# Decoding float64 weights in an attention and feed-forward kernel: magnitudes made in the final weight tile, low words converted on GpSimd

## The chip, the cores and the metric

The kernel runs on one core of a Trainium2 chip. The metric is the device time of one execution in microseconds; the time before is the median of three runs. A core has five engines that work in parallel, each through its own queue in order: TensorE (PE, with its weight loads PEld), VectorE (DVE), ScalarE (ACT), GpSimd (POOL) and SyncE (SP), which here starts the DMA transfers. They wait for each other on semaphores.

## What is computed

Attention over 8 batches of 8 heads, 576 positions, head dimension 64, that keeps for each query the 32 largest scores; then, on the 4608 rows that it gives, a feed-forward layer with an ELU.

```python
scores = scale * np.matmul(q, k.transpose(0, 1, 3, 2))
kth = np.partition(scores, -top_k, axis=-1)[..., -top_k:-top_k + 1]
mask = scores >= kth
...
attn = np.exp(scores)
attn = attn / (np.sum(attn, axis=-1, keepdims=True) + 1e-09)
...
h = x @ w_in
g = np.where(h > 0.0, h, alpha * (np.exp(np.minimum(h, 0.0)) - 1.0))
return (g @ w_out).astype(np.float32)
```

q, k and v are float32. The weights w_in (512 x 2048) and w_out (2048 x 512) come as float64, which the engines do not compute in: the kernel reads each weight as two 32-bit words and makes a float32 of them.

## The kernel before

*Attention.* The work is cut into steps; a step is one tile of 128 queries and one pair of heads. For each, PE makes the scores (L299), ACT copies them to a tile `sc` (L307), and DVE finds the 32 largest by four MAX8 and three MATCH_REPLACE8 per head (L318 to L328, in later steps L341 to L353). POOL makes two small numbers from the result, the neg and gap pair (L366, L368), ACT masks with them (Prelu, L369) and takes the exponential with its sum (L370). POOL normalises: five small instructions (L380 to L385), then two that scale the tile (L387). PE turns the normalised tile (L406), ACT copies the turned parts to `et` (L407), PE multiplies with v (L432), ACT copies the result to `xT` (L459).

*Feed-forward.* The rows are gathered in blocks of one to three tiles of 128 rows. A block has 16 hidden pieces (PE L504 with w_in; ACT L514, L517, L519; DVE L476 closes the ELU) and four projection pieces per tile (PE L529 with w_out). `feed` hands these pieces out among the attention steps by a plan of due times, and holds a piece back until as many weight pieces are decoded as it needs.

*Decoding.* The weights are cut into 32 pieces of 128 x 512, 16 of w_in, then 16 of w_out. A piece is loaded by SP into a `raw` tile of 1024 words (L153; seven buffers), low and high words in turn. Then, before the change:

- ACT L174 copies the low words to floats in place, times 2^-35 plus 2^17: the low word's top three bits become the last bits of the float.
- ACT L175 writes the sign of the value, as an 8-bit float, into the top byte of each low word.
- ACT L178 takes the absolute value of the high word, read as a float, times 2^-62, in place.
- POOL L179 clips that between two bounds, in place.
- DVE L186 shifts the high word left by three bits, in place.
- POOL L187 adds low and high words as integers into the final tile, `w_in` or `w_out`.

The first four are in `convert_first`, the last two in `convert_last`, called three pieces later. `decode_piece(i)` also issues the load of piece i + 3. The selection on DVE calls `hook` after MAX8s (L330, L354), four times per step, and each call runs one decode piece; so the 32 pieces and the three calls that empty the pipeline are spread over the first nine steps. A raw buffer is free for a new load once its piece's add is done, seven pieces earlier.

*Order.* In the first eight steps (`n < tight`) a scheduler orders the instructions of each engine; the start before them and everything after them keeps the order in which it is written. So the decoding lies in the part whose order the scheduler chooses, and a change to it can change the order of other work there too.

Of the kernel before, what the change touches and what calls it, by code (L numbers as in the profile page):

```python
# [8 lines left out]
AF = mybir.ActivationFunctionType  # L9
ALU = mybir.AluOpType  # L10
FP32 = mybir.dt.float32
U32 = mybir.dt.uint32
I32 = mybir.dt.int32
# [68 lines left out]
def kernel(  # L82
# [9 lines left out]
    nc = tc.nc  # L92
# [9 lines left out]
    NF = dff // P  # L102
# [3 lines left out]
    scale = 1.0 / float(D) ** 0.5  # L106
# [33 lines left out]
    raw = {}  # L140

    def weight(i):
        per = dff // WN
        if i < NC * per:
            f, c = divmod(i, NC)
            src = moe_w_in[c * P : (c + 1) * P, 2 * f * WN : 2 * (f + 1) * WN]
            return src, w_in[:, c, f * WN : (f + 1) * WN]
        f = i - NC * per
        return moe_w_out[f * P : (f + 1) * P, :], w_out[:, f, :]

    def load_weight(i):
        t = rawpool.tile([P, 2 * WN], U32, tag="raw", name="raw")
        nc.sync.dma_start(t[:], weight(i)[0])  # L153
        raw[i] = t

    def parts(t):
        words = t[:].rearrange("p (n w) -> p n w", w=2)
        signs = t[:].bitcast(FP8).rearrange("p (n w) -> p n w", w=8)
        return words[:, :, 0], words[:, :, 1], signs[:, :, 3]

    def convert_first(i):

        lo, hi, sign = parts(raw[i])
        ef, mf = hi.bitcast(FP32), lo.bitcast(FP32)
        nc.scalar.activation(mf, lo, AF.Copy, scale=2.0**-35, bias=2.0**17)  # L174
        nc.scalar.activation(  # L175
            sign, ef, AF.Sign, scale=2.0**64, bias=1.0, saturate=False
        )
        nc.scalar.activation(ef, ef, AF.Abs, scale=2.0**-62)  # L178
        nc.gpsimd.tensor_scalar(  # L179
            ef, ef, (2.0 - 2.0**-3 - 2.0**-23) * 2.0**-46, 2.0**-77, ALU.min, ALU.max  # L180
        )

    def convert_last(i):
        t, dst = raw.pop(i), weight(i)[1]
        lo, hi, sign = parts(t)
        nc.vector.tensor_single_scalar(hi, hi, 3, ALU.logical_shift_left)  # L186
        nc.gpsimd.tensor_tensor(  # L187
            dst.bitcast(I32), hi.bitcast(I32), lo.bitcast(I32), ALU.add
        )

    decode = []
    decoded = [0]
# [10 lines left out]
            late["x"] = ctx.enter_context(tc.tile_pool(name="xt", bufs=2))  # L203

    def decode_piece(i):
        if i < 2 * NF:
            if i + 3 < 2 * NF:
                load_weight(i + 3)
            convert_first(i)
        if i > 2:  # L210
            convert_last(i - 3)
            decoded[0] = i - 2

    loaded, kqT, vT = {}, {}, {}

# [342 lines left out]
    for b in range(B):  # L558
# [12 lines left out]
        for qt in range(J + 1):  # L571
# [8 lines left out]
            t = Tile(b, qt, rows, blk, slice(c0, c0 + n))  # L580
# [66 lines left out]
    for hp in range(1, NHP):  # L647
        load_v(0, hp)
    decode += [lambda i=i: decode_piece(i) for i in range(2 * NF + 3)]
    at(0, start_qk, 0, 2)  # L650
    at(1, start_qk, 0, 3)
# [93 lines left out]
```

## Time and profile before

| | us |
|---|---|
| median of three runs | 1667.17 (1666.97 to 1669.18) |
| the profiled execution | 1667.02 |
| its span, first to last instruction | 1665.2 |
| PE busy in the span | 1592.8 (96%) |
| DVE busy | 1495.8 (90%) |
| ACT busy | 1165.1 (70%) |
| POOL busy | 630.5 (38%) |
| mean granted TensorE clock | 0.977 of full speed |

A busy share is an average over stages with different limits. In the first 150 us weights are decoded, the granted TensorE clock lies between 0.5 and 1.0, and PE and DVE have gaps; in the 1400 us after that both are busy almost throughout; at the end PE works alone. Where a line of the trace gives a start and a length, both are in microseconds from the start of the span; `x2` is two instructions in a row, `[2.41 <-DVE m L328]` says that the engine sat idle for 2.41 us before it and that the DVE instruction of line 328 on tile `m` ended the wait. A line of a tile's instructions gives the shortest, median and longest duration in ns, then the first and last start. A line of stages gives the bounds of the stage, its length, the busy time of each engine with its number of instructions, the granted TensorE clock, the busy share of the DMA engines and what they moved in GB/s.

### The profile page before, as it was taken

The numbers are of one execution on the slowest core, as the hardware profiler recorded it, in microseconds if no ns is written. First come the engines' busy times: TensorE is split into PE (matmuls) and PEld (weight loads), VectorE is DVE, ScalarE is ACT, GpSimd is POOL, SyncE is SP. The second block draws the span as 40 slices with busy tenths as digits, with TensorE's granted clock in tenths as the row PEclk, the third lists the DMA queues.
The fourth block names the chain that finished last, engine by engine and source line by source line (L and its number), as shares of the span: only waits on it lengthen the run. The fifth ranks groups of instructions, "written<-read, shape, count | busy, mean of one in ns | idle before, by whom it ended". The sixth has DMA issues, their size and how long they took to land.

```text
span 1665.2 us, 25986 instructions
## 1 busy us (share of the span) xinstructions
PE 1592.8 (96%) x8528; PEld 1031.5 (62%) x8528; DVE 1495.8 (90%) x3044; ACT 1165.1 (70%) x2377; POOL 630.5 (38%) x1719
## 2 busy tenths in 40 slices
PE   5589999999999999999999999999999999999999
PEld 3366677657574767656566676755557575755565
DVE  5887999999999999999999999999999999998500
ACT  6998777668686777678667685868758585857521
POOL 3775444333334334333334333333333343332200
PEclk9578999999999999999999999999999999999999
DMA  7540120001100110001100111001200100000000
GB/s 211 171 144 7 23 50 29 7 15 44 48 1 8 43 42 22 1 28 37 42 14 1 50 29 35 1 14 43 50 13 1 28 15 29 7 7 7 7 13 13
DMA packets 101126, 56.21 MB, mean 34 GB/s; under 512 B 84096, under 2 KB 92288, under 8 KB 100992
## 3 DMA queue, kind: packets, MB, share of 16 engines
q1 hardware_dynamic: 99792, 54.26, 11.7%
q8 instruction: 68, 1.11, 0.3%
q14 instruction: 66, 0.54, 0.1%
q10 hardware_dynamic: 1200, 0.30, 0.1%
HBM read 45.09 MB, written 9.44 MB: 33 GB/s over the span
## 4 chain that ended last, share of the span: by engine, by line
PE 65%; DVE 21%; ACT 9%; POOL 3%; issue 2%; SPq 0%; DMA 0%; ACTq 0%; POOLq 0%; DVEq 0%
PE ops L529 24%; PE hps L504 20%; DVE wk L346 9%; DVE m L353 8%; PE avps L432 7%; PE scps L299 6%; PE eps L406 5%; DVE m L341 3%; ACT sc L370 2%; ACT sc L369 1%; DVE gT L476 1%; ACT raw L175 1%; PE qkps L269 1%; ACT et L407 1%; POOL w_in L187 1%
## 5 line engine op out<-in xcount | busy, mean ns | idle before, releaser
L353 DVE MAX8 m<-wk 128x8 f32<-128x576 f32 x816 | 577.0, 750 | 0.0
L504 PE MATMUL hps<-xT,w_in 128*128 128x256 f32 (+2 forms) x2432 | 548.1, 374 | 12.5 <-ACT xT L459 12.3
L529 PE MATMUL ops<-w_out,gT 128*128 128x512 f32 x1152 | 522.8, 598 | 0.0
L504 PEld LDWEIGHTS hps<-xT,w_in 128*128 128x128 f32 x2432 | 406.5, 193 | 109.2 <-issue 23.8
L346 DVE MATCH_REPLACE8 wk<-m,wk 128x576 f32<-128x576 f32 x544 | 400.8, 746 | 0.0
L529 PEld LDWEIGHTS ops<-w_out,gT 128*128 128x128 f32 x1152 | 208.7, 190 | 233.0 <-issue 219.5
L380 POOL TENSOR_SCALAR dene<-den 128x2 f32<-128x2 f32 x144 | 35.9, 249 | 771.2 <-ACT sc L370 770.6
L369 ACT ACTIVATE sc<-sc,neg 128x576 f32<-128x576 f32 x288 | 226.8, 788 | 89.2 <-POOL neg L366 89.0
L370 ACT ACTIVATE sc<-sc,gap 128x576 f32<-128x576 f32 x288 | 224.1, 778 | 25.7 <-ACT sc L369 0.7
L387 POOL TENSOR_SCALAR sc<-sc,rec 128x576 f32<-128x576 f32 x288 | 221.0, 778 | 14.9
L307 ACT ACTIVATE sc<-scps 128x576 f32<-128x576 f32 x288 | 174.0, 659 | 73.3 <-PE scps L299 73.3
L299 PE MATMUL scps<-kqT 64*128 64x288 f32 (+1 forms) x1280 | 201.8, 440 | 21.2 <-ACT kqT L275 7.9
L407 ACT COPY et<-eps 128x512 f32<-128x512 f32 x288 | 166.8, 579 | 55.2 <-PE eps L406 55.0
L346 DVE MATCH_REPLACE8 wk<-m,sc 128x576 f32<-128x576 f32 x272 | 200.4, 746 | 0.0
L432 PE MATMUL avps<-et,vT 128*64 128x256 f32 (+2 forms) x2080 | 193.3, 326 | 4.8 <-ACT et L407 4.6
L406 PEld LDWEIGHTS eps<-ident,sc 128*128 128x128 f32 x1152 | 143.6, 144 | 83.8 <-issue 46.2
L476 DVE SCALAR_TENSOR_TENSOR gT<-n,gT 128x512 f32<-128x512 f32 (+1 forms) x132 | 100.2, 759 | 102.0 <-ACT n L519 101.9
L341 DVE MAX8 m<-sc 128x8 f32<-128x576 f32 x272 | 191.8, 748 | 0.0
L406 PE MATMUL eps<-ident,sc 128*128 128x128 f32 x1152 | 175.7, 278 | 15.4 <-POOL sc L387 13.0
L432 PEld LDWEIGHTS avps<-et,vT 128*64 128x64 f32 x2080 | 122.6, 141 | 79.1 <-issue 22.8
L299 PEld LDWEIGHTS scps<-kqT 64*128 64x128 f32 (+1 forms) x1280 | 108.1, 181 | 91.9 <-issue 44.2
L514 ACT ACTIVATE n<-hps 128x512 f32<-128x512 f32 (+1 forms) x156 | 88.0, 564 | 71.4 <-PE hps L504 67.5
(47 smaller groups left out, 1170.2 us busy)
## 6 DMA issues: line engine op xcount, KB each, us to landing
kin<-in_k_dram SPq DMA_DIRECT2D x64, 128.0 KB, 2.8
raw<-in_moe_w_in_dram SPq DMA_DIRECT2D x16, 512.0 KB, 5.4
vT<-in_v_dram SPq DMA_DIRECT2D x64, 128.0 KB, 2.3
raw<-in_moe_w_out_dram SPq DMA_DIRECT2D x16, 512.0 KB, 3.9
out_dram<-osb SPq DMA_DIRECT2D x32, 256.0 KB, 2.3
qin<-in_q_dram SPq DMA_DIRECT2D x62, 128.0 KB, 2.8
kin<-in_k_dram SPq DMA_DIRECT2D x32, 32.0 KB, 2.4
vT<-in_v_dram SPq DMA_DIRECT2D x64, 16.0 KB, 2.2
```

Source lines behind the costliest of these rows:

```text
L299: nc.tensor.matmul(wide[i][rows, half, 0:HS], kq[part, q0 : q0 + u.t.ql], kq[part, k0 : k0 + HS], start=True, stop=True,)
L341: nc.vector.max(found[i], cur[i])
L346: nc.vector.match_replace(wk[i], found[i], cur[i], TAKEN)
L353: nc.vector.max(found[i], cur[i])
L369: nc.scalar.activation(sc, sc, AF.Prelu, bias=neg[:], alpha=STEEP)
L370: nc.scalar.activation(sc, sc, AF.Exp, bias=gap[:], accum_out=u.den[:, i : i + 1])
L387: nc.gpsimd.tensor_scalar(u.sc[:, i, :], u.sc[:, i, :], rec[:, i : i + 1], 1.0, ALU.mult, ALU.mult)
L406: nc.tensor.transpose(ps[:, c * P : (c + 1) * P], sc[:, c0 : c0 + P], ident[:])
L407: nc.scalar.copy(g.et[:, chunks, u.at, :], ps[:, 0 : n * P].rearrange("p (c q) -> p c q", c=n),)
L432: nc.tensor.matmul(ps[i * D : (i + 1) * D, cols], vt[:, 2 * J + i if c == J else i * J + c, :], w, start=(c == 0), stop=(c == J),)
L504: nc.tensor.matmul(blk.h[:, f % bank, :], w_in[:, i, f * P : (f + 1) * P], blk.xT[:, i, 0:n_tok], start=(i == 0), stop=(i == NC - 1),)
L529: nc.tensor.matmul(blk.o[:], blk.gT[f // NG][:, f % NG, s * P : (s + 1) * P], w_out[:, f, :], start=(f == 0), stop=(f == NF - 1),)
```

## The change

The copy of the low words leaves ACT: POOL converts them, with the same scale and offset, by a `tensor_scalar` that reads unsigned integers and writes floats in place. Abs, on ACT, reads the high words (every second word of `raw`) and writes the magnitudes to the final weight tile, 512 words in a row; the clip on POOL and the shift on DVE then work in place there, and the last add on POOL adds the low words to it. Sign is still on ACT and still writes into the low word, which POOL has converted first. The four parts of a piece are four stages, each called one decode piece after the one before; the add still comes three pieces after the first stage. Per piece, ACT has two instructions where it had three, POOL three where it had two, DVE one as before. Loads, buffers and the number of decode pieces that a feed-forward piece waits for are the same.

```diff
-        lo, hi, sign = parts(raw[i])
-        ef, mf = hi.bitcast(FP32), lo.bitcast(FP32)
-        nc.scalar.activation(mf, lo, AF.Copy, scale=2.0**-35, bias=2.0**17)
+        lo, hi, _ = parts(raw[i])
+        nc.scalar.activation(weight(i)[1], hi.bitcast(FP32), AF.Abs, scale=2.0**-62)
+        nc.gpsimd.tensor_scalar(
+            lo.bitcast(FP32), lo, 2.0**-35, 2.0**17, ALU.mult, ALU.add
+        )
+
+    def convert_second(i):
+        _, hi, sign = parts(raw[i])
+        w = weight(i)[1]
+        nc.gpsimd.tensor_scalar(
+            w, w, (2.0 - 2.0**-3 - 2.0**-23) * 2.0**-46, 2.0**-77, ALU.min, ALU.max
+        )
         nc.scalar.activation(
-            sign, ef, AF.Sign, scale=2.0**64, bias=1.0, saturate=False
+            sign, hi.bitcast(FP32), AF.Sign, scale=2.0**64, bias=1.0, saturate=False
         )
-        nc.scalar.activation(ef, ef, AF.Abs, scale=2.0**-62)
-        nc.gpsimd.tensor_scalar(
-            ef, ef, (2.0 - 2.0**-3 - 2.0**-23) * 2.0**-46, 2.0**-77, ALU.min, ALU.max
-        )
+
+    def convert_third(i):
+        w = weight(i)[1].bitcast(U32)
+        nc.vector.tensor_single_scalar(w, w, 3, ALU.logical_shift_left)
 
     def convert_last(i):
-        t, dst = raw.pop(i), weight(i)[1]
-        lo, hi, sign = parts(t)
-        nc.vector.tensor_single_scalar(hi, hi, 3, ALU.logical_shift_left)
-        nc.gpsimd.tensor_tensor(
-            dst.bitcast(I32), hi.bitcast(I32), lo.bitcast(I32), ALU.add
-        )
+        w, t = weight(i)[1].bitcast(I32), raw.pop(i)
+        nc.gpsimd.tensor_tensor(w, w, parts(t)[0].bitcast(I32), ALU.add)
...
     def decode_piece(i):
-        if i < 2 * NF:
-            if i + 3 < 2 * NF:
-                load_weight(i + 3)
-            convert_first(i)
-        if i > 2:
-            convert_last(i - 3)
-            decoded[0] = i - 2
+        stages = (convert_first, convert_second, convert_third, convert_last)
+        if i + 3 < 2 * NF:
+            load_weight(i + 3)
+        for ago, stage in enumerate(stages):
+            if 0 <= i - ago < 2 * NF:
+                stage(i - ago)
+        decoded[0] = max(0, i - 2)
```

## The prediction

> **What bounds the kernel now.** I read the busy time by stage first, then the rows of the raw weight tiles, then POOL's own timeline, then PE's where its last long gap ends. The stages are cut at POOL's first normalisation (31.3 us), its second (54.0), its seventh (129.4), and where PE stops waiting (136.6). Columns: PE, PEld, DVE, ACT, POOL busy us (count), PE clock, DMA share, GB/s.
>
> ```profile
> 31.30:54.00 22.70, 9.09 (x53) 6.40 (x53) 17.61 (x38) 20.40 (x35) 13.17 (x24) 0.67 0.62 219
> 54.00:129.40 75.40, 58.98 (x298) 44.73 (x299) 60.26 (x124) 73.42 (x127) 56.41 (x97) 0.65 0.50 152
> 129.40:136.60 7.20, 3.08 (x22) 2.03 (x20) 1.12 (x2) 7.20 (x14) 5.43 (x10) 0.88 0.00 1
> 136.60:1560.00 1423.40, 1405.11 (x7755) 909.44 (x7756) 1389.24 (x2829) 1017.52 (x2118) 538.20 (x1540) 1.00 0.09 23
> 1560.00:1665.20 105.20, 101.06 (x345) 58.21 (x343) 12.35 (x22) 26.66 (x52) 9.14 (x26) 0.99 0.04 13
> ```
>
> From 136.6 to the end PE is busy 1506.2 of 1528.6 us, on work that this change does not touch. So a shift of PE's restart at 136.6 passes to the end one for one, and the change is worth only what it moves before that. There ACT sets the pace: 73.42 of 75.40 us in the long stage, while POOL has 19.0 us free.
>
> The weight pieces (32, of 128x512) cost, in ns min/median/max:
>
> ```profile
> L174 ACT ACTIVATE raw<-raw x32: 651/708/857, 8.7 to 138.8; 128x512 f32<-128x512 uint32 x32
> L175 ACT ACTIVATE raw<-raw x32: 1327/1402/1589, 9.3 to 140.4; 128x512 fp8e4<-128x512 f32 x32
> L178 ACT ACTIVATE raw<-raw x32: 639/724/922, 10.8 to 142.2; 128x512 f32<-128x512 f32 x32
> L179 POOL TENSOR_SCALAR raw<-raw x32: 638/658/923, 11.5 to 143.3; 128x512 f32<-128x512 f32 x32
> L186 DVE TENSOR_SCALAR raw<-raw x32: 401/429/1281, 12.2 to 148.1; 128x512 uint32<-128x512 uint32 x32
> L187 POOL TENSOR_TENSOR w_in<-raw x16: 1032/1038/1301, 12.8 to 82.8; 128x512 int32<-128x512 int32 x16
> ```
>
> POOL over one step of four pieces, start and length in us:
>
> ```profile
> 68.96 0.23 POOL L380 TENSOR_SCALAR dene<-den 128x2 f32<-128x2 f32 x1
> ...
> 70.92 1.48 POOL L387 TENSOR_SCALAR sc<-sc,rec 128x576 f32<-128x576 f32 x2
> 72.36 0.23 POOL L366 TENSOR_SCALAR neg<-m 128x1 f32<-128x1 f32 x1
> 72.56 0.19 POOL L368 TENSOR_TENSOR gap<-m,m 128x1 f32<-128x1 f32 x1
> 72.84 1.64 POOL L179 TENSOR_SCALAR raw<-raw 128x512 f32<-128x512 f32 x2
> 74.55 1.04 POOL L187 TENSOR_TENSOR w_in<-raw 128x512 int32<-128x512 int32 x1
> 75.96 1.04 POOL L187 TENSOR_TENSOR w_in<-raw 128x512 int32<-128x512 int32 x1 [0.37 <-DVE raw L186]
> 79.41 0.21 POOL L366 TENSOR_SCALAR neg<-m 128x1 f32<-128x1 f32 x1 [2.41 <-DVE m L328]
> 79.85 1.62 POOL L179 TENSOR_SCALAR raw<-raw 128x512 f32<-128x512 f32 x2
> 81.55 2.27 POOL L187 TENSOR_TENSOR w_in<-raw 128x512 int32<-128x512 int32 x2
> ```
>
> A normalisation occupies POOL from 68.96 to 72.40 (3.45 us), a neg and gap pair 0.45. Packed, a clip (L179) takes 0.85 with its gap (72.84 to 74.55 for two), an add (L187) 1.17 (79.85 and 81.55: two of each in 4.05), though alone they take 0.66 and 1.04. The next normalisation follows at 83.90.
>
> PE's restart:
>
> ```profile
> 133.10 0.60 PE L406 MATMUL eps<-ident,sc 128*128 128x128 f32 x4
> 136.56 2.28 PE L299 MATMUL scps<-kqT 64*128 64x288 f32 x6 [2.86 <-ACT et L407]
> ```
>
> It waits for ACT's copy of the seventh normalised tile, which stands behind two pieces' work on ACT.
>
> **The change, part by part.** *Removed from ACT:* 32 copies. In pairs they start 0.57 apart (1.13 for two in the chain of waits at 74.87), so some 18 us leave ACT, 11 of them (20 pieces) in the long stage. ACT no longer sets the pace there. *Moved within ACT:* Abs writes the final tile; same size, priced as L178. Sign now waits for POOL's conversion, since it writes into the word that is converted; masks, score evictions and et copies queue behind it, and PE and DVE wait for those. In the changed order of instructions ACT's Signs from the fourteenth piece on need no wait of their own: a conversion that ACT has waited past earlier covers them. So I price the wait at nothing while POOL keeps up; if POOL is late, it is in POOL's terms. *Clip and shift* work on contiguous words: a clip takes 0.66 for 512 strided values, the scaling of 576 contiguous ones (L387) 0.74 each, the same per value, so no gain; the shift keeps 0.43, hidden by DVE's 15 us of idle time in the stage. *DMA:* the same 32 loads on SP; each still waits for the add that frees its buffer.
>
> *Added on POOL:* 32 conversions. No row shows POOL reading unsigned integers into floats. Below stands L179 (same instruction, stride and count), 0.66 alone and 0.85 packed; above, POOL's other integer row, the add, at 1.17 packed. I take 0.85, the nearer row.
>
> On the dtype, the Trainium skill (GPSIMD: programming the Q7 cores, SBUF Data Layout) says that with conversion on, every element passes a float32 converter on the read port even when it is float32 already. By that rule an integer input costs nothing extra and the total below stands; by the add's row it would be about 9 us more.
>
> On sharing, it says (GPSIMD Engine Reference, Key points) that GpSimd and VectorE contend when VectorE runs in a two-port mode. The rows show something of the kind: L186 takes 0.43 alone and 1.27 where an add runs (59.63, 74.60), and the second of two clips stretches to 0.92. By the rule conversions suffer too, as the packed 0.85 has it; were they spared (0.72, L179's mean), 28 of them would give back 3.6 us.
>
> Now the sum, along POOL's queue in the changed order.
>
> 1. *Start.* The copy of the second piece (13.04 to 13.75) and part of the chain ahead of the first scores goes; POOL converts beside ACT: -0.6 (0 to -1.3).
> 2. *First to second normalisation*, 22.7 us now, with ACT full from 36.7. POOL is free at 35.7; before its second normalisation then stand 6 conversions, 5 clips, 4 adds, one pair: 6 x 0.85 + 5 x 0.85 + 4 x 1.17 + 0.45 = 14.5, to 50.2 against 54.0: -3.8. With means (0.72, 1.11) it is 12.8 and -5.5; none if other waits hold.
> 3. *Five intervals to the seventh normalisation*, 53.98 to 129.44 = 75.5 us. POOL's queue holds 22 conversions, 20 clips, 20 adds, 5 normalisations, 10 pairs: 22 x 0.85 + 20 x 0.85 + 20 x 1.17 + 17.25 + 4.5 = 80.9: +5.4. Lowest: today's busy 56.4 plus 22 x 0.72 = 72.3: -3.2. Highest, conversions at 1.17: +12.4.
> 4. *Loads.* A conversion waits for a load which waits for the add seven pieces earlier, on the same queue. Between the two stand 4.7, 3.9, 4.2 and 3.3 us of POOL work for pieces 26, 27, 30 and 31; a load needs 0.33 to issue and 3.9 to land. Short by 1.4; with hand-overs I take +2.0 (0 to 7, with the 5.4 landing of the w_in loads).
> 5. *POOL's own waits.* In the stage it now waits 7.9 us for DVE (L328, L186) and 7.5 for ACT. The latter go with ACT's load; of the former I leave a third, +2.6 (0 to 7.9).
> 6. *Exit.* With ACT free, the last et copy starts 4.90 after a normalisation begins (31.29 to 36.19); at the end of the stage it takes 6.81 (129.44 to 136.25): -1.9 (0 to -1.9).
>
> Sum: -0.6 - 3.8 + 5.4 + 2.0 + 2.6 - 1.9 = +3.7. The profiled execution took 1667.0 us (span 1665.2, 1.8 around it), 0.2 under the median of 1667.2. Prediction: 1670.7, rounded 1671. The last w_out adds come some 10 us of POOL work (4 clips, 5 adds, 2 pairs) after the seventh normalisation; PE needs them for its last block-0 products, at 154.1 now, which covers them. SP's loads of the next q and k queue behind the raw loads, but are used some ten steps later.
>
> **Rivals.**
>
> *POOL keeps up: faster.* The mechanism is POOL's packed price of conversions and clips. Break-even of the total lies where 42 of them in term 3 cost 3.7 us less, 0.76 each. Below that ACT's relief wins. For it: alone they take 0.66, and 19.0 us of POOL idle time stand against 22 x 0.72 = 15.9. Against it: every packed pair in the timeline costs 0.85 a piece. With means throughout and no waits the sum is -0.6 - 5.5 - 3.2 - 1.9 = -11; halfway to break-even, 1661.
>
> *Integer input is dear: clearly slower.* At the add's 1.17, 28 conversions cost 9.0 more: 1680. For it: the only integer row on POOL is the slow one; against: that row has two inputs. Two passes (2.34) would give 1712.
>
> *It cancels.* Without terms 4 and 5 the sum is -0.9: 1666, within the bound of no change; with half of them, 1668. For it: POOL's new load nearly equals ACT's old one.
>
> **How the numbers follow.** What a measurement of this kernel can tell from no change is about 0.2%, 3.3 us. Forecast (moderately slower, 1670.5 to 1677): 0.30. Integer input dear: 0.20. Cancels: 0.26. POOL keeps up: 0.24. So slower 0.50, same 0.26, faster 0.24. The likeliest is 1671; its own range is 1668 to 1677. Both signs hold weight, so the full range reaches from the middle of the faster case, 1660, past the dear-integer case with some of term 4's upper bound, 1687.
>
> **What would show it.** Right: in the stretch between second and seventh normalisation POOL is busy over 90% and ACT under 90%; conversions appear near 0.7 to 0.85; the second normalisation starts near 50, the seventh near 136, PE restarts near 140. Wrong: conversions over 1 us (integer case), or a POOL still idle a fifth of the stretch with ACT busy (then ACT was not the pace), or a PE that starts its unbroken work before 133 (POOL kept up). It would also be wrong if PE's work after the restart changes in length, which I put at nothing: the order of its instructions there is the same.

## The result, and the profile after

The changed kernel takes 1675.61 us (median of five, 1675.36 to 1677.62), the kernel before in the same series 1669.18 (1666.97 to 1669.41); the ratio is 1.0047 with a 95% interval of 1.0033 to 1.0062, so it is slower by 0.47%, 7.8 us. In this series the executions of either kernel fall into two groups some 2 us apart, and the two profiled ones are not of the same group (10.2 us apart), so times are compared by ratios and not by two single values. The profiled execution took 1677.26 us, span 1675.5.

The stages of the changed kernel, cut at the same events as before (second, seventh normalisation, PE's restart), and a later stretch. Columns: PE, PEld, DVE, ACT, POOL busy us (count), PE clock, DMA share, GB/s.

```profile
30.08:54.02 23.94, 11.32 (x53) 7.04 (x53) 14.88 (x32) 17.21 (x30) 16.88 (x27) 0.66 0.63 217
54.02:138.15 84.13, 59.31 (x303) 44.10 (x304) 55.18 (x116) 63.66 (x106) 76.33 (x119) 0.63 0.43 135
138.15:143.11 4.96, 2.58 (x17) 1.54 (x15) 4.96 (x11) 4.96 (x9) 4.36 (x9) 1.00 0.00 0
...
165.00:700.00 535.00, 519.95 (x3271) 360.58 (x3268) 535.00 (x1096) 389.55 (x815) 207.65 (x606) 0.99 0.10 26
```

In the long stage POOL is now the full engine, 76.33 of 84.13 us (91%), and ACT has room, 63.66. The stage grew from 75.46 to 84.13. Lines of the file after the conversions stand five lower than before (L380 is L385).

| event | before | predicted | after |
|---|---|---|---|
| first normalisation | 31.29 | 30.7 | 30.08 |
| second | 53.98 | near 50 | 54.02 |
| seventh | 129.44 | near 136 | 138.15 |
| PE's restart | 136.56 | near 140 | 143.11 |

The weight pieces after, in ns min/median/max, then the first and last start:

```profile
L174 POOL TENSOR_SCALAR raw<-raw x32: 637/668/1087, 8.6 to 136.1; 128x512 f32<-128x512 uint32 x32
L181 POOL TENSOR_SCALAR w_in<-w_in x16: 612/613/615, 9.3 to 84.7; 128x512 f32<-128x512 f32 x16
L184 ACT ACTIVATE raw<-raw x32: 1319/1347/1379, 9.2 to 153.6; 128x512 fp8e4<-128x512 f32 x32
L190 DVE TENSOR_SCALAR w_in<-w_in x16: 410/426/428, 9.9 to 85.4; 128x512 uint32<-128x512 uint32 x16
L194 POOL TENSOR_TENSOR w_in<-w_in,raw x16: 1279/1287/1531, 10.7 to 91.9; 128x512 int32<-128x512 int32 x16
```

The conversion (L174) costs what the clip did before (0.658). The clip is a little cheaper, 0.613, and in this kernel no longer stretches to 0.9. The add is dearer: 1.287 against 1.038, by mean 1.37 against 1.09, which the prediction did not foresee.

Between the first two normalisations, PE, ACT and POOL in turn (start, length, what it is, idle time before it):

```profile
32.85 0.69 PE L411 MATMUL eps<-ident,sc 128*128 128x128 f32 x2 [5.10 <-POOL sc L392]
33.47 2.29 PE L304 MATMUL scps<-kqT 64*128 64x288 f32 x8
...
35.79 1.19 ACT L312 ACTIVATE sc<-scps 128x576 f32<-128x576 f32 x2 [4.56 <-PE scps L304]
36.87 1.08 ACT L412 COPY et<-eps 128x512 f32<-128x512 f32 x2
...
39.61 0.66 ACT L173 ACTIVATE w_in<-raw 128x512 f32<-128x512 f32 x1
...
34.39 0.66 POOL L174 TENSOR_SCALAR raw<-raw 128x512 f32<-128x512 uint32 x1
40.35 0.61 POOL L181 TENSOR_SCALAR w_in<-w_in 128x512 f32<-128x512 f32 x1 [5.30 <-ACT w_in L173]
```

PE's scores now stand behind two turns of the normalised tile, which wait 5.10 us for POOL; ACT waits 4.56 for those scores (2.02 before), its first Abs of the interval starts at 39.61, behind score and `et` copies (its first decode instruction stood at 36.67 before), and POOL idles 5.30 for that Abs. From 40.35 on POOL works without a wait to 54.02.

And POOL in the long stage, ahead of a neg and gap pair:

```profile
97.18 0.61 POOL L181 TENSOR_SCALAR w_out<-w_out 128x512 f32<-128x512 f32 x1
97.87 1.53 POOL L194 TENSOR_TENSOR w_out<-w_out,raw 128x512 int32<-128x512 int32 x1
99.38 0.64 POOL L174 TENSOR_SCALAR raw<-raw 128x512 f32<-128x512 uint32 x1
99.98 1.27 POOL L194 TENSOR_TENSOR w_out<-w_out,raw 128x512 int32<-128x512 int32 x1
101.23 0.20 POOL L371 TENSOR_SCALAR neg<-m 128x1 f32<-128x1 f32 x1
```

POOL stands between DVE's search and ACT's mask in every step: a neg of 0.20 us comes after 4.05 us of decoding that POOL does without a pause, and ACT's mask waits 1.91 us for it. That is one form in which POOL's load reaches the other engines. The waits for the clip, the normalised tile and the neg between 30 and 165 us (total, times, longest), before and after:

```profile
DVE raw L186 <- POOL raw L179: 22.3, 17, 4.0
PE eps L406 <- POOL sc L387: 13.0, 5, 3.4
ACT sc L369 <- POOL neg L366: 3.2, 2, 2.5
...
DVE w_in L190 <- POOL w_in L181: 22.7, 13, 5.0
PE eps L411 <- POOL sc L392: 22.4, 7, 5.1
ACT sc L374 <- POOL neg L371: 15.8, 11, 3.5
DVE w_out L190 <- POOL w_out L181: 15.5, 12, 3.0
```

The last four are the changed kernel's largest waits in that stretch, PE's weight loads aside: all for POOL.

### The profile page after: what moved, and what is told of

Same layout as the page of the kernel before. It is cut to its first block, busy times and chain, and to the rows that moved or that the text cites. A ratio compares the mean times of both kernels' runs of the same rounds, so it can differ in the third digit from the quotient of the medians.

```text
span 1675.5 us, 25943 instructions
## 1 busy us (share of the span) xinstructions
PE 1597.1 (95%) x8528; PEld 1032.4 (62%) x8528; DVE 1495.6 (89%) x3044; ACT 1149.9 (69%) x2345; POOL 659.2 (39%) x1751
## 3 DMA queue, kind: packets, MB, share of 16 engines
q8 instruction: 68, 1.11, 0.3%
## 4 chain that ended last, share of the span: by engine, by line
PE 70%; DVE 16%; ACT 6%; POOL 5%; issue 2%; DMA 1%; SPq 0%; ACTq 0%; POOLq 0%; DVEq 0%
PE ops L534 25%; PE hps L509 22%; PE avps L437 8%; PE scps L304 7%; DVE wk L351 7%; DVE m L358 6%; PE eps L411 5%; DVE m L346 2%; ACT sc L375 1%; ACT sc L374 1%; PE qkps L274 1%; POOL raw L174 1%; DVE gT L481 1%; POOL sc L392 1%; ACT et L412 1%
## 5 line engine op out<-in xcount | busy, mean ns | idle before, releaser
L385 POOL TENSOR_SCALAR dene<-den 128x2 f32<-128x2 f32 x144 | 36.2, 251 | 788.0 <-ACT sc L375 787.7
```

## The experiments

The theory after this reading: POOL has become the pacing engine of the decoding, through the conversions. Rivals: the new place of the magnitudes, with the dearer add, is the cost; the four staggered stages and the order that the scheduler makes of them are the cost. All ratios are to the kernel before, which ran beside each series (medians 1667.4 to 1667.7).

**Conversion back on ACT (e1).** Diff to the changed kernel:

```diff
+        nc.scalar.activation(lo.bitcast(FP32), lo, AF.Copy, scale=2.0**-35, bias=2.0**17)
         nc.scalar.activation(weight(i)[1], hi.bitcast(FP32), AF.Abs, scale=2.0**-62)
-        nc.gpsimd.tensor_scalar(
-            lo.bitcast(FP32), lo, 2.0**-35, 2.0**17, ALU.mult, ALU.add
-        )
```

> The changed kernel with the low words' conversion put back on ACT (its old Copy); magnitudes stay in the final tile, four stages stay. Theory (POOL paces the decode stage, mainly by the conversions' 0.67 us each): POOL loses 22 x 0.67 = 15 us in the long stage, ACT sets the pace again as before, the adds stay at 1.29 but lie beside ACT; about 1667 to 1670. Rival 'layout' (the add at 1.29 instead of 1.04 and the work in the final tile are the cost, not the conversions): 1673 to 1677, as the changed kernel. Rival 'staging' (the four staggered stages and the scheduler's order of the entry cost the time): second normalisation at 54 and slower than 1672 too.

1666.24 us, ratio 0.9990 (0.9981 to 0.9999). The whole loss goes with this one instruction's move, though the adds stay dear (median 1.293 us for w_in, 1.520 for w_out) and the second normalisation comes nearly as late after the first (23.3 us, 23.94 in the changed kernel, 22.69 before). In that kernel ACT is busy 76.00 of the 76 us from 54 to 130. So the layout and the stages alone are not the cost.

**Conversion on POOL, magnitudes in raw (e2).** The changed kernel with the conversion alone in the first stage, Sign and Abs in the second, all in `raw`, and the add as before:

```diff
-        w, t = weight(i)[1].bitcast(I32), raw.pop(i)
-        nc.gpsimd.tensor_tensor(w, w, parts(t)[0].bitcast(I32), ALU.add)
+        t, dst = raw.pop(i), weight(i)[1]
+        lo, hi, _ = parts(t)
+        nc.gpsimd.tensor_tensor(
+            dst.bitcast(I32), hi.bitcast(I32), lo.bitcast(I32), ALU.add
+        )
```

> Conversion on POOL as in the changed kernel, but magnitudes stay in the raw tile (both inputs of the add strided as in the kernel before, output to the final tile). ACT's Sign and Abs follow the conversion by one stage. Theory: the add is back at 1.04, 20 adds in the long stage give 5.0 us back, 32 give 8; so 1667 to 1671, with the seventh normalisation at 131 to 134. Rival 'conversions alone' (their 0.67 each is the cost and the add's price lies beside other work): 1674 to 1677, seventh normalisation at 137 or later.

1674.16 us, ratio 1.0039 (1.0027 to 1.0052). The adds are back at 1.040 us, POOL has some 7 us less work in all (the clips cost a little more again), and the time stays within the interval of the changed kernel's: the conversions alone make nearly all of the loss. My theory, which gave the add 5 to 8 us, had that part wrong, although its mark on the stage was met: the seventh normalisation starts at 133.79. The second starts at 50.57, near where the prediction had it, and the loss is there all the same. Why 7 us less on POOL bring so little was not isolated.

**The price of the add by its operands (e3).** One execution, 1684.17 us; only the adds of its diff are shown:

```diff
+        if i % 4 == 0:
+            nc.gpsimd.tensor_tensor(w, w, lo, ALU.add)
+        elif i % 4 == 1:
+            nc.gpsimd.tensor_tensor(w, lo, w, ALU.add)
+        elif i % 4 == 2:
+            nc.gpsimd.tensor_tensor(lo, w, lo, ALU.add)
+            nc.vector.tensor_copy(w, lo)
+        else:
+            nc.gpsimd.tensor_tensor(w, hi, lo, ALU.add)
```

> One look for the price of the add by the places of its operands, eight pieces each: w+lo to w (as the changed kernel), lo+w to w (operands exchanged), w+lo to lo in raw (with a copy to w by DVE behind it), hi+lo both from raw to w (as the kernel before). If working in place is dear: the first three at 1.28, the last at 1.04. If one contiguous and one strided input is dear, the same, but then the second or third differ from the first by operand or output: a first operand that is contiguous costing 1.28 and a second that is contiguous 1.04 would show that the order decides. If the output's place decides, the third is cheap or dear alone. The time itself says nothing.

```profile
L202 POOL TENSOR_TENSOR w_in<-w_in,raw x4: 1285/1410/1533, 11.1 to 80.2; 128x512 int32<-128x512 int32 x4
...
L204 POOL TENSOR_TENSOR w_in<-raw,w_in x4: 1291/1302/1472, 15.6 to 81.4; 128x512 int32<-128x512 int32 x4
...
L206 POOL TENSOR_TENSOR raw<-w_in,raw x4: 1286/1288/1310, 27.0 to 83.8; 128x512 int32<-128x512 int32 x4
...
L209 POOL TENSOR_TENSOR w_in<-raw x4: 1034/1124/1216, 47.0 to 93.3; 128x512 int32<-128x512 int32 x4
```

The shortest of each form: 1.285, 1.291, 1.286 and 1.034. Neither the operands' order nor the output's place decides: one contiguous and one strided input cost 1.29, two strided inputs from one tile 1.03. Whether two contiguous inputs would be cheap was not tried.

**The conversions left out (e4).** The three lines of the conversion are taken out.

> The changed kernel without the low words' conversion: it is left out, so the weights' low bits are not those of the reference. Neither ACT nor POOL does it. Theory (POOL paces): POOL 22 x 0.67 = 15 us lighter in the long stage, ACT at 56 of 75 busy; the stage is shorter than before by 5 to 12 us, 1656 to 1663 in all. Rival 'staging': the stage does not become shorter than before's 75.5 us, 1668 or more.

1665.77 us, ratio 0.9991 (0.9982 to 1.0000): only 1.5 us faster than before, although from 54 to 130 no engine is near full (PE 56.1, DVE 61.6, ACT 66.3, POOL 60.6 of 76). The theory's 5 to 12 us are a miss. Of the 'staging' rival the mark on the stage is met, its time is not: from the second to the seventh normalisation this kernel takes 75.73 us, before 75.46, and what it gains lies ahead of that (the second normalisation starts at 50.19). So without the conversions the stage is 8.4 us shorter than in the changed kernel, but no shorter than before. One place of the stage, POOL, then ACT:

```profile
68.06 0.62 POOL L178 TENSOR_SCALAR w_in<-w_in 128x512 f32<-128x512 f32 x1
68.76 1.55 POOL L191 TENSOR_TENSOR w_in<-w_in,raw 128x512 int32<-128x512 int32 x1
70.40 0.61 POOL L178 TENSOR_SCALAR w_in<-w_in 128x512 f32<-128x512 f32 x1
71.09 0.47 POOL L368 TENSOR_SCALAR neg<-m 128x1 f32<-128x1 f32 x1
...
71.60 0.78 ACT L371 ACTIVATE sc<-sc,neg 128x576 f32<-128x576 f32 x1 [2.56 <-POOL neg L368]
```

ACT idles 2.56 us for a neg that stands behind three decode instructions on POOL. The stage is a ring of hand-overs (search on DVE, neg on POOL, mask on ACT, normalisation on POOL, turn on PE, copy on ACT). I read the result so: each hand-over queues behind decoding, and taking load off an engine that is not full shortens little. No run shows this by itself.

**How much POOL bears (e6, e7).** Conversions shared between the two engines, in e1's place; in e7 pieces 0, 4, 8 and so on convert on POOL, a quarter of them:

```diff
+        if i % 2:        # e7: i % 4
+            nc.scalar.activation(lo.bitcast(FP32), lo, AF.Copy, scale=2.0**-35, bias=2.0**17)
+        else:
+            nc.gpsimd.tensor_scalar(lo.bitcast(FP32), lo, 2.0**-35, 2.0**17, ALU.mult, ALU.add)
```

> Every second conversion on ACT, the others on POOL, all else as the changed kernel. Between all on ACT (1666.2) and all on POOL (1675.6). If the cost is in proportion to the conversions on POOL: 1671. If POOL costs nothing until it is nearly full (68 of 75 us busy with all of them, 63 with none): 1664 to 1667, with ACT at about 66 of 75.

> Three of four conversions on POOL, the fourth pieces' ones... read as written: pieces 0, 4, 8, ... convert on POOL, all others on ACT; all else as the changed kernel. In proportion: 1668.5. If the best balance of ACT and POOL lies between: 1662 to 1666, faster than all on ACT.

| on POOL | median, us | ratio (95%) | ACT, POOL busy of 76 us (54 to 130) |
|---|---|---|---|
| none (e1) | 1666.24 | 0.9990 (0.9981 to 0.9999) | 76.0, 63.6 |
| 8 of 32 (e7) | 1666.98 | 0.9997 (0.9988 to 1.0006) | 73.1, 62.4 |
| 16 of 32 (e6) | 1668.36 | 1.0002 (0.9994 to 1.0011) | 68.4, 66.3 |
| 32 (changed) | 1675.61 | 1.0047 (1.0033 to 1.0062) | 55.9, 68.9 |

The first 16 cost 2.0 us (0.0012 of 1667; the two intervals still overlap), the second 16 cost 7.5. So the cost is not in proportion, which gave 1671 for e6: most of it comes with the second half, where POOL is busiest. e6 lies a little above the 1664 to 1667 of its other expectation. There is no gain over e1 at any share; e7's second expectation is a miss.

**The last conversions alone on POOL (e12).** As e1, with `if i < 27` on ACT.

> As the run with the conversions on ACT (1666.2), but those of the last five pieces (27 to 31) on POOL. Between 125 and 145 us ACT was 19.6 of 20 us busy there and POOL 13.0, so POOL has room where ACT has none. If ACT sets the pace of the stage's last part: two to three conversions less ahead of ACT's copies for PE's restart, 1.4 to 2.1 us, so 1664 to 1665. If the hand-overs between the engines set it, and not ACT's load: 1665.5 to 1667.5, no gain.

1668.30 us, ratio 1.0003 (0.9994 to 1.0012): no gain over e1; the time lies even a little above the second expectation's 1665.5 to 1667.5. Relief of a full ACT, bought with POOL's time, does not shorten this stage.

**The clip on DVE (e5).** In `convert_second`:

```diff
-        nc.gpsimd.tensor_scalar(
+        nc.vector.tensor_scalar(
             w, w, (2.0 - 2.0**-3 - 2.0**-23) * 2.0**-46, 2.0**-77, ALU.min, ALU.max
         )
```

> The changed kernel with the clip of the magnitudes on VectorE instead of GpSimd (same words, same place); nothing is left out. POOL loses 20 x 0.62 = 12 us in the long stage, and DVE's shift no longer waits for POOL (in the changed kernel DVE waits 38 us for the clips between 30 and 165). DVE gains 32 clips; at the shift's 0.43 that is 14 us of work. Theory (the end follows DVE: DVE's idle time up to 145 us plus its decode work, since DVE never idles from there to 700): idle falls from 39 to 10-20 us and work rises by 14, so 1660 to 1672, and the end's difference to before equals the two changes to within 2 us. Rival (POOL's busy time alone paces): as with the conversions left out, 1664 to 1667, seventh normalisation at 126.

1671.56 us, ratio 1.0025 (1.0016 to 1.0034): about half of the loss goes, at the upper edge of the theory's range. The rival's 1664 to 1667 is refuted. DVE is the busiest engine now (70.2 of 76 us, POOL 58.7), but that is not where the rest of the loss lies: in the profiled execution the search of DVE's tenth step starts at 146.89, earlier than before (148.47). The seventh normalisation is as late as in the changed kernel (137.47), PE's turns wait 11.59 us for it, PE then works without a wait, and DVE waits 4.7 us for the hidden piece that ACT gets from PE:

```profile
141.59 1.12 PE L411 MATMUL eps<-ident,sc 128*128 128x128 f32 x4 [11.59 <-POOL sc L392]
146.89 1.42 DVE L346 MAX8 m<-sc 128x8 f32<-128x576 f32 x2 [0.31 <-POOL gap L373]
...
DVE gT L481 <- ACT n L524: 4.7, 1, 4.7
```

**The shift one piece later (e10).**

```diff
-        if i + 3 < 2 * NF:
-            load_weight(i + 3)
-        for ago, stage in enumerate(stages):
+        if 0 < i < 2 * NF - 2:
+            load_weight(i + 2)
+        for ago, stage in zip((0, 1, 3, 4), stages):
...
-        decoded[0] = max(0, i - 2)
+        decoded[0] = max(0, i - 3)
...
```

> The changed kernel with DVE's shift one piece later and the add another, and the loads two pieces ahead instead of three (seven raw tiles hold no more). In the changed kernel DVE waits 38 us for POOL's clips between 30 and 165. If that wait at the head of DVE's queue is what passes to the end, most of the loss goes: 1667 to 1671. If POOL's own load is it (68 of 75 us busy, unchanged here), DVE waits elsewhere instead: 1674 to 1678.

1673.96 us, ratio 1.0039 (1.0027 to 1.0052). DVE's waits for the clips fall from 38.2 to 27.0 us between 30 and 165, and the time by 1.3 by the ratios, within their intervals. That is at the lower edge of the second range: the wait at the head of DVE's queue looks like a symptom of POOL's load more than a cause.

**The stages alone (e11).** The kernel before, its operations on their engines and in `raw`, spread over the four stages.

```diff
         nc.scalar.activation(ef, ef, AF.Abs, scale=2.0**-62)
+
+    def convert_second(i):
+        ef = parts(raw[i])[1].bitcast(FP32)
         nc.gpsimd.tensor_scalar(
             ef, ef, (2.0 - 2.0**-3 - 2.0**-23) * 2.0**-46, 2.0**-77, ALU.min, ALU.max
         )
...
+    def convert_third(i):
+        _, hi, _ = parts(raw[i])
+        nc.vector.tensor_single_scalar(hi, hi, 3, ALU.logical_shift_left)
...
```

> The kernel before with its operations on its engines and its raw layout, only spread over four stages as in the changed kernel (clip one piece later, shift two, add three). Tells whether the small gain of the run with the conversions on ACT (1666.2 against 1667.4) is the stages' or the final tile's. If the stages': 1665 to 1666.5. If the final tile's: 1667 to 1669, as before. The add at 1.04 instead of 1.29 could make it better still, 1663 to 1665.

1668.54 us, ratio 1.0007 (0.9998 to 1.0016): the stages change nothing that can be told. Against it e1 (0.9990), whose magnitudes are in the final tile, gains about 2.8 us by the ratios, even with the dearer add; the intervals touch, so this gain is likely, not shown.

**Whose delay reaches the end (e8, e9).** The prediction passed PE's restart on to the end. Both edits are made to the kernel before, in the step with `n == 10` (the eleventh), just behind the stage:

```diff
         next(passes)
+        for _ in range(11 if n == 10 else 0):
+            nc.vector.max(cur.first[:, 0, :], cur.sc[:, 0, :])
         feed(n, 0.25)
```

```diff
-        for c in range(n):
+        for c in list(range(n)) * times:
...
-            turn(done, main)
+            turn(done, main, 15 if n == 10 else 1)
```

> The kernel before with 11 more MAX8 in step 10 (the same search of the same row, its result written again): 11 x 0.75 = 8.2 us of VectorE, just behind the decode stage (about 165 us). Prediction's step ('a delay of PE's restart passes to the end one for one; PE is the pace from there'): PE has all its other work, DVE has 20 us of waits later, so 1667 to 1670. Theory now (DVE, which never idles from 139 to 700 us, hands its delay on): 1674 to 1676.

> The kernel before with 14 more passes over four transposes in step 10, the same products written again: 56 x 0.15 = 8.4 us of TensorE at about 170 us. Prediction's step (PE is the pace): 1675 to 1676. Theory now (DVE is the pace up to 700 us, PE has some 14 us of waits between 139 and 700): PE takes up most of it, 1667 to 1671.

The added work of e8, on DVE:

```profile
160.22 8.70 DVE L690 MAX8 m<-sc 128x8 f32<-128x576 f32 x11
```

and of e9, on PE, with DVE's only wait from 160 to 400 us:

```profile
163.74 6.71 PE L406 MATMUL eps<-ident,sc 128*128 128x128 f32 x60
...
174.39 0.69 DVE L476 SCALAR_TENSOR_TENSOR gT<-n,gT 128x512 f32<-128x512 f32 x1 [3.85 <-ACT n L519]
```

e8 takes 1676.54 us, ratio 1.0053 (1.0041 to 1.0066), 8.8 us more: all of DVE's 8.7 reaches the end, and the prediction's step (1667 to 1670) is refuted. e9 takes 1671.04, ratio 1.0023 (1.0013 to 1.0032), 3.8 us more: PE's added work is 6.71 - 0.60 = 6.1 us (I had put it at 8.4), and what reaches the end is the 3.85 us that DVE had to wait for it. So just behind the stage DVE hands its delay to the end, and PE only what it makes DVE wait.

The start of DVE's tenth and twenty-sixth step (first MAX8) and the last instruction, in one profiled execution each, against before's 148.5, 309.9 and 1665.2:

| kernel | tenth step | twenty-sixth | end |
|---|---|---|---|
| changed | +9.2 | +9.3 | +10.3 |
| e1 conversion on ACT | -2.3 | -2.3 | -1.7 |
| e2 conversion on POOL, raw | +7.0 | +7.0 | +7.6 |
| e3 forms of the add | +16.2 | +16.2 | +16.9 |
| e4 no conversion | -2.1 | -2.1 | -1.6 |
| e5 clip on DVE | -1.6 | +3.2 | +3.3 |
| e6 half | -0.4 | -0.3 | -0.2 |
| e7 quarter | -1.1 | -0.7 | -0.1 |
| e8 more DVE | +0.8 | +9.5 | +9.7 |
| e9 more PE | +1.4 | +5.4 | +5.8 |
| e10 shift later | +4.9 | +4.9 | +5.3 |
| e11 stages alone | +0.8 | +0.8 | +1.6 |
| e12 last conversions | +1.7 | +2.1 | +2.5 |

In every one of them the end follows DVE's twenty-sixth step within 1.0 us, and in e5 and e9 the wait after the tenth step (4.7 and 3.85 us) stands between the two columns. e8 and e9 are the kernel before up to the tenth step and read +0.8 and +1.4 there, so a difference of that size means nothing in this table. POOL's seventh normalisation, which the prediction followed, tells less: it starts 8.0 us late in e5, 4.4 late in e2 and 8.7 late in the changed kernel, against -1.6, +7.0 and +9.2 for DVE's tenth step.

## Why the prediction was right in sign, and where it fell short

The forecast was slower, 1671 with a range up to 1687; it came to 1675.6. The cause, the conversion's move from ACT to POOL, is shown: undoing this move alone ends the loss (e1), keeping it alone keeps the loss (e2). That POOL's load is how it works is supported: POOL is busy 91% of the stage, and taking the clips off it instead (e5) brings DVE's tenth step back as well. The way from POOL to the end was not the one that the prediction added up, and that its number came as near as it did is in part luck (term 3). By its own steps, in the profiled executions:

1. *Start*, -0.6: measured -1.2. Right.
2. *First to second normalisation*, -3.8: measured +1.2 (22.69 to 23.94). This is the term that is furthest off: "POOL is free at 35.7; before its second normalisation then stand 6 conversions, 5 clips, 4 adds, one pair: [...] to 50.2 against 54.0: -3.8". The work was sized about right, 13.7 us from 40.35 to 54.02 for all but the first conversion. But POOL could not start on it: it waited 5.30 us for ACT's Abs, which stood behind score copies that the scheduler's new order had put behind PE's turns. I took the old queue of ACT for the new one. The 5.0 us between -3.8 and +1.2 are more than the whole miss of 4.6. But no run shows that they reach the end: e1 has nearly the same interval (23.3 us) and no loss, e2 has a short one (20.47) and the loss.
3. *Five intervals*, with terms 4 and 5: +5.4, +2.0, +2.6 = +10.0: measured +8.7 (75.46 to 84.13). The sum is near, and term 3 by chance: from each start on POOL's timeline in this stage to the next, without its waits, an add takes 1.41 for 1.17 (20 of them: +4.9), a clip 0.694 for 0.85 (-3.1) and a conversion 0.72 for 0.85 (-2.9 for the 22 expected; there are 23). The prediction put the add at its old price and the other two at that of a stretched strided pair. POOL's waits in the stage are 0.6 us for loads (term 4 said +2.0) and 1.6 for ACT (term 5: +2.6, for DVE): both terms were too large.
6. *Exit*, -1.9: measured -2.2 (7.12 to 4.96). Right, and for the reason given: ACT's copy comes sooner.

These make +6.5 at PE's restart (136.56 to 143.11) where +3.7 stood. The step after them failed: "a shift of PE's restart at 136.6 passes to the end one for one". In the profiled executions +6.5 at the restart became +10.3 at the end: from its restart to the end PE took 1532.4 us where it took 1528.6, so the prediction's last mark of being wrong is met there. (By the ratio of all runs the whole is 7.8, so how much comes behind the restart in other executions stays open.) The window from 136.6 to 1560 had PE at 1405.11 and DVE at 1389.24 of 1423.40 us, and I took the larger. Cut shorter, the kernel before reads otherwise:

```profile
140.00:700.00 560.00, 546.58 (x3380) 374.25 (x3377) 560.00 (x1148) 406.22 (x846) 222.38 (x634) 1.00 0.10 25
```

DVE does not pause once in 560 us, while PE has 13.4 us of gaps. The Trainium skill (Perfetto Trace Analysis, Identifying the Most-Contended Engine) says that TensorE's matmul busy share is a poor measure of how near it is to its limit, while VectorE's occupancy is a fair one; e8 and e9 fit that, 8.8 us more for 8.7 added on DVE and 3.8 more for 6.1 added on PE, though PE's busy share was the larger. The beginning of DVE's unbroken work and its tenth step, before and after:

```profile
138.53 0.69 DVE L476 SCALAR_TENSOR_TENSOR gT<-n,gT 128x512 f32<-128x512 f32 x1 [3.42 <-ACT n L519]
148.47 1.41 DVE L341 MAX8 m<-sc 128x8 f32<-128x576 f32 x2
...
145.06 0.43 DVE L190 TENSOR_SCALAR w_out<-w_out 128x512 uint32<-128x512 uint32 x1 [1.22 <-POOL w_out L181]
157.71 1.41 DVE L346 MAX8 m<-sc 128x8 f32<-128x576 f32 x2
```

DVE's last wait ends 6.5 us later too, but 12.65 us of its work then stand ahead of the tenth step where 9.94 stood before: DVE, held up by POOL in the stage (busy 75.8 of the 115 us from 30 to 145, 86.8 before), has more left to do. So the tenth step is 9.2 us late, and the end follows DVE.

On the rivals: *POOL keeps up* is refuted, and not by the packed price: its break-even, 0.76 for conversions and clips, was met (0.72 and 0.70). Its condition left out the dearer add and what DVE still has to do. *Integer input is dear* is refuted: 0.668 against 0.658 for the same instruction on floats. That agrees with the rule from the Trainium skill (GPSIMD: programming the Q7 cores, SBUF Data Layout), by which a float32 input passes the converter too. *It cancels* is met by e6, with half of the conversions moved, and not by the change.

Sign's new wait, priced at nothing, is 1.3 us on ACT in all; right. The loads of w_out and the last adds (155.16) hold nobody up at the restart; right. One gap in PE's work after the restart: at 197.6 PE waits 2.82 us (0.53 before) for ACT's kqT copy, which stands behind a mask that waits for a POOL neg, and that for DVE's late search.

No version tried beats the kernel before by more than 0.2%. The lowest is e1, 0.9990 (0.9981 to 0.9999): the change without its conversion's move.

What stays open: by which hand-over POOL's load holds DVE up most, which part of the ring of hand-overs sets the floor near 146 us for DVE's tenth step (e1 146.2, e4 146.3, e5 146.9, with different engines full), why e2's lighter POOL gains so little, and how much of the loss would go with another order of the first eight steps.

## What to carry to other kernels

Be careful with filling an engine that passes small results between others (here POOL with its 0.2 us neg): half of the moved work was nearly free, the other half cost 7.5 us, and a sum of busy times shows neither. When a part of the program is ordered by a scheduler, take an interval's price from the new order of all engines, the waits of the engine ahead included, and not from the receiving engine's queue alone; and ask whether the end of that interval is what later work waits for. Here POOL's normalisations were not: in e5 the seventh came 8.0 us late and DVE's tenth step 1.6 early. To see whose delay reaches the end, look for the engine that has no pause in the stretch just behind the change, by windows short enough that a later stage does not hide it.

## What the hardware did that was not expected

GpSimd's integer add of 128 x 512 words takes, at its shortest, 1.03 us with both inputs at every second word of one tile and 1.29 with one contiguous input, whatever the order or the output's place. The Trainium skill (GPSIMD Engine Reference, Elementwise — side-by-side cycle accounting) gives two-input operations one price, about 2.6 cycles an element at 1.2 GHz (from a float32 add), an estimate of 1.11 us here; the runs show two, and they decide. A clip of contiguous words keeps 612 to 618 ns in the changed kernel, where the strided one went from 638 to 923; in e1 it goes up to 896. The shift on DVE, up to 1281 ns before, stays at 520 or less in the changed kernel, but reaches 1459 again in e1 with the same layout; what it collides with there was not isolated.
